# The fifth row tile of layer 2 in two column halves of 64 rows, with the next 64 rows behind a branch

## The chip, the cores and the metric

The kernel runs on one core of one Trainium2 chip. The metric is the device time of that core in microseconds; before the change it is 227.52 us, the median of three runs (227.28 to 228.74). The profile is of one further execution, whose span is 224.6 us; positions in time are counted from the start of that span.

## The reference

Two stages follow each other. The first is a linear attention over q, k and v of shape 8 x 8 x 576 x 64 (batch, heads, positions, width): q is softmaxed over its width, k over its positions, and the result is q (k^T v) for each head. The second takes the 4608 rows of 512 numbers that come out and sends each through one of eight experts, picked by a hash of its token:

```
q_s = exp(q - max(q, -1)) ; q_s /= sum(q_s, -1)
k_s = exp(k - max(k, 2))  ; k_s /= sum(k_s, 2)
kv  = einsum('bhsd,bhse->bhde', k_s, v)
x   = einsum('bhsd,bhde->bhse', q_s, kv)      -> 4608 rows of 512
expert_idx = token_ids * 2654435761 % 8
out[rows of e] = max(x[rows of e] @ w1[e], 0) @ w2[e]      (512 -> 1024 -> 512)
```

The rows of an expert are known only from the data. The inputs are one seeded draw, in which the eight experts get 631, 561, 550, 592, 536, 584, 564 and 590 rows.

## The kernel before, in words

**Attention and sorting.** For each of the eight batches the kernel loads q, k and v, exponentiates on ScalarE, forms k^T v and the attention rows on TensorE, scales them on VectorE into xn, and then sorts the rows by expert: one-hot matrices built on VectorE (line 609) multiply the rows on TensorE (619), and GpSimd copies the segments into xT (653). Each expert has room for 640 rows in xT (CAP), in two halves of 320 (H2). Which output row belongs to which slot is worked out on VectorE (lines 430 to 477; selA and selB are the operands), and a chain of 40 matmuls at line 834 sums it into an index table idx. Should an expert have more rows than fit, a flag sends all engines into a second copy of the computation, the fallback, which stands behind one branch per engine at line 154; with this draw it isn't run.

**The experts.** `layer1` (695) computes hT = relu(xT^T w1) for two of eight 128-row chunks of the hidden width at a time, for one half of the rows: 8 matmuls, into two PSUM banks out of banks 0 to 5 (`lslot`). The first half is always 320 columns wide; in the second the width of the matmul is a shape register that holds the expert's count less 320, cut to between 32 and 320 (`widths`, `load_widths`). The relu out of PSUM is on ScalarE (702) or VectorE (704). `layer2` (721) takes 128 rows of hT as the stationary operand and all 512 columns of w2 as the moving one, and sums eight chunks of the hidden width into one bank, 6 or 7 in turn: 8 matmuls of 128x512. Five such row tiles, t = 0 to 4, make an expert. The first four cover rows 0 to 511; the fifth covers rows 512 to 639, of which only the first (count - 512) hold data. `rows_out` copies a tile from PSUM to yo, on ScalarE for even t (731) and on VectorE for odd t (733), for expert 0 always on ScalarE. `store` (739) sends the 128 rows to their places in the output with one indirect DMA from GpSimd; slots without a row have an index beyond the output and are dropped.

**What sets the order.** The program is written out by hand as one list of operations per engine; each engine works its list in order. `Emit.op` collects what an operation reads (R), writes (W) and writes in part (P), works out which other engines' semaphores it must wait for, places these waits ahead of the operation's first instruction, and lets its last instruction count up its engine's semaphore. W waits for all earlier writers and readers, P for readers only. TensorE doesn't wait for itself. For each expert ee, TensorE's list reads: layer 1 of expert ee+1, two units of its first half; layer 2 of ee, five tiles; then the six other units of layer 1 of ee+1. Expert 1's layer 2 has the index table's matmuls ahead of it. The stores of the last expert come after GpSimd's branch at line 154.

So layer 2 of tile t waits for the copy of tile t - 2 out of the same bank: `layer2` writes one bank alone.

Of the kernel before, what the change touches and what calls it, by code (L numbers as in the profile page):

```python
# [9 lines left out]
ACTF = mybir.ActivationFunctionType  # L10
# [154 lines left out]
def fused_kernel(nc, q, k, v, moe_token_ids, moe_w1, moe_w2, out):  # L165
    B, H, S, DH = q.shape
    NTOK = moe_token_ids.shape[0]
    E, D, F = moe_w1.shape
    assert (B, H, S, DH, E, D, F) == (8, 8, 576, 64, 8, 512, 1024) and NTOK == B * S
    NC = 9  # L170
    T = 5
# [6 lines left out]
    H2 = CAP // 2  # L178
    CAPS = CAP + SEG[0]
    FC = F // 128  # L180
    NYO = 13

    em = Emit(nc)
# [4 lines left out]
    def at(name, shape, dt, off=None):  # L188
        size = {F32: 4, BF16: 2, F16: 2, I32: 4, I64: 8}[dt]
        for n in shape[1:]:  # L190
            size *= n
        size = (size + 31) // 32 * 32
        if off is None:
            off = cur[0]
            cur[0] += size
        return nc.alloc_sbuf_tensor_at(name, shape, dt, offset=off)
# [21 lines left out]
    hT = [at("hT%d" % i, [128, FC, CAP], BF16) for i in range(2)]  # L218
# [3 lines left out]
    w1b, w2b, wreg = [], [], [qkv0, qkv0 + 18432, qkv0 + 36864, exp0]  # L222
# [3 lines left out]
    NW = len(wreg)  # L226
    yo = [at("yo%d" % i, [128, D], F32, xn0 + 2048 * ((i - 1) % NYO)) for i in range(NYO)]
# [43 lines left out]
    PB = nc.alloc_psum_tensor("ps", [128, 8, 512], F32)  # L271
    PBH = PB[:].rearrange("p b x -> p (b x)").bitcast(BF16)
    bk = [Buf() for _ in range(8)]
# [4 lines left out]
    def dv(fn, R=(), W=(), P=()):  # L278
        em.op("dve", fn, R, W, P)

    def ac(fn, R=(), W=(), P=()):
        em.op("act", fn, R, W, P)
# [31 lines left out]
    for h in range(2):  # L314
        for a in range(2):
# [8 lines left out]
       R=[b_tok], P=[b_ei])  # L324
# [7 lines left out]
        out=flg[:], in0=e_f[:].rearrange("p b (g t) -> p (b g) t", t=TG).unsqueeze(2).to_broadcast(gs4),  # L332
        in1=iota8[:].unsqueeze(1).unsqueeze(3).to_broadcast(gs4), op=ALU.is_equal),
       R=[b_ef2, bc["iota8"]], W=[b_flg])
# [5 lines left out]
          R=[b_flg, bc["upper"], bc["ones"]], W=[bk[6], bk[7]])  # L340
# [13 lines left out]
       R=[b_pr], W=[b_pos])  # L354
# [55 lines left out]
           W=[b_wd])  # L410
        gp(lambda e: e.tensor_copy(out=widei[:], in_=wide[:]), R=[b_wd], W=[b_wi])

    shp = []

    def load_widths():
        def ld(e):
            rs = [e.alloc_register("wd%d" % i) for i in range(E)]
            e.load(rs, widei[0:1, :])
            shp.extend(e.shape_register(i) for i in range(E))
            for h in range(2):  # L420
                e.move_shape(shp[4 * h:4 * h + 4],
                             [[(1, e.snap(r, min_val=32, max_val=H2))] for r in rs[4 * h:4 * h + 4]])
        em.raw("pe", ld, R=[b_wi])
# [235 lines left out]
    b_w2 = [Buf() for _ in range(NW)]  # L659
    b_hT = [[[Buf() for _ in range(FC // 2)] for _ in range(2)] for _ in range(2)]  # L660
    b_yo = [Buf() for _ in range(NYO)]
# [3 lines left out]
    def weights1(ee, s, R=()):  # L665
        for a in range(2):
            em.dma("pool", "d_w1_%d" % s, lambda e, a=a: e.dma_start(
                w1b[s][64 * a:64 * a + 64, :, :],
                moe_w1[ee].rearrange("(a g p) f -> a p g f", a=2, g=4)[a]), R=R,
                W=([b_w1[s]] if a == 0 else ()), P=(() if a == 0 else [b_w1[s]]))  # L670
# [13 lines left out]
    def weights2(ee, s):  # L684
        for a in range(2):
            em.dma("pool", "d_w2_%d" % s, lambda e, a=a: e.dma_start(  # L686
                w2b[s][:, 4 * a:4 * a + 4, :],
                moe_w2[ee].rearrange("(c p) d -> p c d", p=128)[:, 4 * a:4 * a + 4, :]),
                W=([b_w2[s]] if a == 0 else ()), P=(() if a == 0 else [b_w2[s]]))
# [17 lines left out]
    lsl, ysl, yev = [0], [0], [0]  # L707

    def lslot():
        lsl[0] += 1  # L710
        return 2 * ((lsl[0] - 1) % 3)

    def l1(ee, f, hf, u, onact):
        layer1(ee % NW, f, hf, lambda d: xT[:, d, CAPS * ee + H2 * hf:CAPS * ee + H2 * hf + H2],
               [b_xT] if hf == 0 else [b_xT, b_x6, b_x7], ee % 2, u, onact, ee if hf else None,
               b_wf[f // (FC // 2)] if ee == 0 else None)

    def layer2(s, t, hp):
        u = 6 + ysl[0] % 2
        ysl[0] += 1  # L720
        em.op("pe", [lambda e, fc=fc: e.matmul(  # L721
            PB[:, u, :], hT[hp][:, fc, 128 * t:128 * t + 128], w2b[s][:, fc, :],
            start=(fc == 0), stop=(fc == FC - 1)) for fc in range(FC)],
            R=[b_w2[s]] + (b_hT[hp][0] if t < 3 else []) + (b_hT[hp][1] if t > 1 else []), W=[bk[u]])
        return u

    def rows_out(u, onact):
        y = yev[0] % NYO
        yev[0] += 1
        if onact:  # L730
            ac(lambda e: e.activation(yo[y][:], PB[:, u, :], ACTF.Copy), R=[bk[u]], W=[b_yo[y]])  # L731
        else:
            dv(lambda e: e.tensor_copy(out=yo[y][:], in_=PB[:, u, :]), R=[bk[u]], W=[b_yo[y]])  # L733
        return y
# [3 lines left out]
    def store(ee, t, y, after=()):  # L738
        em.dma("pool", "d_o%d" % y, lambda e: e.indirect_dma_start(  # L739
            out=out[:, :], out_offset=IndirectOffsetOnAxis(ap=idx[:, 5 * ee + t:5 * ee + t + 1], axis=0),  # L740
            in_=yo[y][:], in_offset=None, bounds_check=NTOK - 1, oob_is_err=False),
            R=[b_yo[y], b_idx, *after], P=[b_out])
# [88 lines left out]
    def index_table():  # L831
        u = lslot()
        P2 = PB[:, u, 0:2 * B * T]
        em.op("pe", [lambda e, i=i: e.matmul(P2, selA[:, i, :], selB[:, valid[i], :, :].rearrange("p k n -> p (k n)"),
                                             start=(i == 0), stop=(i == B * T - 1)) for i in range(B * T)],
              R=[b_A, b_B], W=[bk[u]])
        dv(lambda e: e.tensor_copy(out=idxf[:], in_=P2[:, B * T:2 * B * T]), R=[bk[u]], W=[b_idf])
        dv(lambda e: e.scalar_tensor_tensor(out=idxf[:], in0=P2[:, 0:B * T], scalar=64.0, in1=idxf[:], op0=ALU.mult,
                                            op1=ALU.add), R=[bk[u]], W=[b_idf])
        dv(lambda e: e.tensor_scalar(out=idxf[:], in0=idxf[:], scalar1=-1.0, scalar2=8192.0, op0=ALU.mult,  # L840
                                     op1=ALU.add), W=[b_idf])

        dv(lambda e: e.tensor_scalar(out=idx[:], in0=idxf[:], scalar1=ov8k[:, 0:1], scalar2=None, op0=ALU.max),
           R=[b_idf, b_ov8], W=[b_idx])
# [6 lines left out]
    for ee in range(E):  # L851
        units = [(f, hf) for hf in range(2) for f in range(0, FC, 2)] if ee > 0 else [(f, 1) for f in range(0, FC, 2)]
        for i, (f, hf) in enumerate(units):
            if i == 2:
                if ee == 1:
                    for key in ("pe", "pool"):
                        em.load_flag(key, ovfi[0:1, 0:1], [b_ovi])
                    index_table()
                for t in range(T):
                    y = rows_out(layer2(ee % NW, t, ee % 2), ee == 0 or t % 2 == 0)  # L860
                    if ee == E - 1:
                        em.after_tail(lambda: store(ee, t, y))
                    elif ee == 1:
                        store(0, t, t, [b_yo[y]])
                        held.append((t, y))
                    elif ee > 1:
                        if held:
                            store(1, *held.pop(0), [b_yo[y]])
                        store(ee, t, y)
                if ee == 0:  # L870
                    weights2(3, 3)
                if ee == E - 2:
                    before_last = dict(em.cnt)
                if 0 < ee < E - 3:
                    weights1(ee + 3, (ee + 3) % NW)
                    weights2(ee + 3, (ee + 3) % NW)
            if ee + 1 < E:
                l1(ee + 1, f, hf, lslot(), ee == 0 or ee == 1 and i < 2 or (f // 2) % 2)
            if ee == 1 and i in (2, 4, 6):
                store(1, *held.pop(0), [b_hT[0][hf][f // 2]])  # L880
# [40 lines left out]
    for t in range(T):  # L921
        dv(lambda e, t=t: e.tensor_copy(out=idt[:, t, 128 * t:128 * t + 128], in_=ident[:]), R=[bc["ident"]],
           W=[b_id])
    for b in range(B):
# [12 lines left out]
        for ch in range(4):  # L937
            u = 2 * (ch % 2)
            em.op("pe", [lambda e, t=t, hf=hf, ch=ch, u=u: e.matmul(
                PB[:, u + hf, 0:H2], xn[0][:, t, 128 * ch:128 * ch + 128], idt[:, t, H2 * hf:H2 * hf + H2],  # L940
                start=(t == 0), stop=(t == T - 1)) for t in range(T) for hf in range(2)],
                R=b_xn[0] + [b_id], W=bk[u:u + 2])
            ac(lambda e, ch=ch, u=u: e.activation(xg[:, ch, :].rearrange("p (h x) -> p h x", h=2),
                                                  PB[:, u:u + 2, 0:H2], ACTF.Copy), R=bk[u:u + 2], W=[b_xg[ch]])
        for ee in range(E):
# [5 lines left out]
            for t in range(T):  # L951
                u = layer2(NW, t, 2)
                m = flg[:, 2 * b + t // TG, ee, t % TG:t % TG + 1]
                if ee == 0:
                    dv(lambda e, t=t, u=u, m=m: e.tensor_scalar(out=yg[:, t, :], in0=PB[:, u, :], scalar1=m,
                                                                scalar2=None, op0=ALU.mult),
                       R=[bk[u], b_flg], W=[b_yg[t]])
                else:
                    dv(lambda e, t=t, u=u, m=m: e.scalar_tensor_tensor(
                        out=yg[:, t, :], in0=PB[:, u, :], scalar=m, in1=yg[:, t, :], op0=ALU.mult, op1=ALU.add),  # L960
                       R=[bk[u], b_flg], W=[b_yg[t]])
# [9 lines left out]
def bass_efficient_attn_shen__then__hash_routing_kernel(nc, q, k, v, moe_token_ids, moe_w1, moe_w2, out):  # L971
    fused_kernel(nc, q, k, v, moe_token_ids, moe_w1, moe_w2, out)
# [28 lines left out]
```

## Time and profile before

| | |
|---|---|
| time | 227.52 us |
| span of the profile | 224.6 us, TensorE at full clock |
| TensorE matmul busy | 193.6 us (86%), 1786 matmuls |
| VectorE / ScalarE / GpSimd busy | 126.0 / 106.4 / 120.4 us |
| layer 2 matmuls (721), 128x512 | 320, in stretches of 40 |
| layer 1 matmuls (695), second half up to 320 wide | 512 |
| a yo copy of 128x512, ScalarE / VectorE | 597 ns / 692 ns, 26 and 14 of them |
| a relu of 128x640, ScalarE / VectorE | 703 ns / 824 ns |

Busy time of the matmuls includes their pipeline: one of 512 columns is shown as 379 ns but the next starts 216 ns after it, and this start-to-start time (the slot) is what a row of them costs. In a line of the timeline the columns are start, length, engine, line, operation, output and inputs; in brackets is how long the engine had stood idle, and what released it. A line of the chain of work has start, length, and engine, tile and line. "PE" is TensorE, "DVE" VectorE, "ACT" ScalarE, "POOL" GpSimd, and "ps" is PSUM.

### The profile page before, as it was taken

Reading aid. Unit: us, or ns where it says so; the run is one execution under the profiler, and the core shown is the slowest. Engines: PE = TensorE matmul, PEld = TensorE weight load, DVE = VectorE, ACT = ScalarE, POOL = GpSimd, SP = SyncE. Lnnn points to the kernel's source line nnn. Section 1 sums busy time; section 2 is a strip of 40 time slices with the busy share of each in tenths; the row PEclk is TensorE's granted clock in tenths of the full one; section 3 lists DMA queues with packets and bytes.
Section 4 is the critical chain, followed back from the end, with each engine's and each line's share of the span. In section 5 each row is a group of like instructions: output and inputs, shape, how many; then the busy total and the mean of one; then the engine's idle time right before and its main releaser. Section 6 shows DMA issues by size and latency. Waiting matters only on the chain.

```text
span 224.6 us, 4635 instructions
## 1 busy us (share of the span) xinstructions
PE 193.6 (86%) x1786; PEld 130.8 (58%) x1788; DVE 126.0 (56%) x276; ACT 106.4 (47%) x133; POOL 120.4 (54%) x226
## 2 busy tenths in 40 slices
PE   0529976967777799999989999999999999999991
PEld 0328665856565667774654854854855845845640
DVE  5777999988898975899932412412421422412220
ACT  3447887888878837673521331331322322322411
POOL 6600658887996999910005857806715615126053
PEclk9999999999999999999999999999999999999999
DMA  5999999999999999999995599999799799113023
GB/s 144 400 392 393 388 390 390 391 391 395 387 390 392 281 176 186 204 210 206 210 208 157 146 191 228 357 192 237 200 207 258 143 206 228 73 40 147 26 93 134
DMA packets 29791, 54.96 MB, mean 245 GB/s; under 512 B 2367, under 2 KB 11583, under 8 KB 29760
## 3 DMA queue, kind: packets, MB, share of 16 engines
q0 software_dynamic: 16544, 26.22, 56.2%
q1 hardware_dynamic: 13216, 28.35, 34.3%
q8 instruction: 16, 0.26, 0.5%
q14 instruction: 15, 0.12, 0.2%
HBM read 61.90 MB, written 10.49 MB: 322 GB/s over the span
## 4 chain that ended last, share of the span: by engine, by line
PE 49%; DVE 21%; DMA 15%; SPq 9%; issue 3%; ACT 1%; POOL 1%; DVEq 0%; POOLq 0%
PE ps L721 26%; PE ps L695 20%; SPq L495 8%; DMA kf<-in_k_dram 7%; DMA vf<-in_v_dram 7%; DVE selA L477 3%; DVE xn L596 3%; DVE vx L514 1%; DMA tok<-in_moe_token_ids_dram 1%; DVE xT L653 1%; DVE oneh L609 1%; DVE selB L465 1%; DVE zz L433 1%; DVE selB L468 1%; ACT ek L509 1%
## 5 line engine op out<-in xcount | busy, mean ns | idle before, releaser
L739 POOL DMA_INDIRECT out_dram<-yo,idx x40 | 39.5, 988 | 75.5 <-ACT yo L731 55.4
L721 PE MATMUL ps<-w2b,hT 128*128 128x512 bf16 x320 | 70.4, 379 | 0.0
L695 PE MATMUL ps<-xT,w1b 128*128 128x320 bf16 (+1 forms) x512 | 64.4, 286 | 0.3 <-DVE xn L596 0.3
L695 PEld LDWEIGHTS ps<-xT,w1b 128*128 128x128 bf16 x512 | 49.8, 98 | 14.5 <-DVE xn L596 0.7
L721 PEld LDWEIGHTS ps<-w2b,hT 128*128 128x128 bf16 x320 | 31.3, 98 | 36.2
L653 POOL COPY xT<-xs x112 | 45.0, 455 | 9.3 <-issue 2.3
L702 ACT ACTIVATE hT<-ps 128x640 bf16<-128x640 f32 x41 | 28.8, 703 | 36.2 <-PE ps L695 35.9
L731 ACT ACTIVATE yo<-ps 128x512 f32<-128x512 f32 x26 | 15.5, 597 | 55.2 <-PE ps L721 55.2
L704 DVE TENSOR_SCALAR hT<-ps 128x640 bf16<-128x640 f32 x23 | 19.0, 824 | 30.2 <-PE ps L695 30.2
L733 DVE COPY yo<-ps 128x512 f32<-128x512 f32 x14 | 9.7, 692 | 44.0 <-PE ps L721 44.0
L619 PE MATMUL ps<-oneh,xn 128*128 128x384 bf16 (+1 forms) x160 | 22.8, 297 | 3.9 <-DVE xn L596 3.9
L596 DVE TENSOR_TENSOR xn<-ps,rq 128x1024 bf16<-128x1024 f32 (+2 forms) x23 | 23.6, 1079 | 3.3 <-PE ps L591 3.3
L505 ACT ACTIVATE eq<-qf 128x1152 bf16<-128x1152 f32 x16 | 17.7, 1156 | 11.3 <-DMA qf<-in_q_dram 11.3
L619 PEld LDWEIGHTS ps<-oneh,xn 128*128 128x128 bf16 x160 | 14.6, 99 | 11.3 <-DVE xn L596 4.7
L626 ACT ACTIVATE xs<-ps 128x768 bf16<-128x768 f32 (+1 forms) x32 | 18.7, 651 | 3.3 <-PE ps L619 2.7
L509 ACT ACTIVATE ek<-kf 128x2304 bf16<-128x2304 f32 x8 | 17.0, 2123 | 6.4 <-DMA kf<-in_k_dram 6.4
L591 PE MATMUL ps<-kvn,qT 128*128 128x128 bf16 x160 | 11.3, 231 | 5.2 <-DVE kvn L555 5.1
L546 PE MATMUL ps<-vx,ek 64*128 64x130 bf16 x252 | 9.4, 229 | 6.5 <-DVE vx L514 6.5
L523 PE MATMUL ps<-ident,eq 128*128 128x128 bf16 x144 | 11.4, 242 | 3.2 <-ACT eq L505 2.3
L591 PEld LDWEIGHTS ps<-kvn,qT 128*128 128x128 bf16 x160 | 9.9, 104 | 6.0 <-DVE kvn L555 5.7
L546 PEld LDWEIGHTS ps<-vx,ek 64*128 64x128 bf16 x252 | 8.3, 100 | 7.9 <-issue 5.2
L686 POOL DMA_DIRECT2D w2b<-in_moe_w_dram x16 | 12.3, 793 | 0.0
(105 smaller groups left out, 139.1 us busy)
## 6 DMA issues: line engine op xcount, KB each, us to landing
qf<-in_q_dram SPq DMA_DIRECT2D x8, 1152.0 KB, 15.5
kf<-in_k_dram SPq DMA_DIRECT2D x8, 1152.0 KB, 15.7
w2b<-in_moe_w_dram POOLq DMA_DIRECT2D x16, 512.0 KB, 11.7
vf<-in_v_dram SPq DMA_DIRECT2D x7, 1152.0 KB, 15.4
w1b<-in_moe_w_dram POOLq DMA_DIRECT2D x14, 512.0 KB, 8.4
vf<-in_v_dram SPq DMA_DIRECT2D x2, 576.0 KB, 14.7
w1b<-in_moe_w_dram POOLq DMA_DIRECT2D x4, 256.0 KB, 6.0
out_dram<-yo,idx POOLq DMA_INDIRECT x40, 3.8
```

The costliest lines, as they stand in the source:

```text
L495: em.dma("sync", nm % p, lambda e, dst=dst, src=src: e.dma_start(dst[p][:].rearrange("p h c d -> p h (c d)"), src[b].rearrange("(a h) (p c ...
L509: ac(lambda e: e.activation(ek[p][:].rearrange("p j c a d -> p a (j c) d"), kf[p][:].rearrange("p (a j) c d -> p a (j c) d", a=2), ACTF.Ex ...
L591: em.op("pe", [lambda e, i=i, j=j, h2=h2: e.matmul(PB[:, bank + i, 256 * j + 128 * h2:256 * j + 128 * h2 + 128], qt(p, t0 + i, j, h2), kvn ...
L596: dv(lambda e: e.tensor_tensor(out=xn[p][:, t0:t0 + n, :].rearrange("p t (g x) -> p (t g) x", x=DH), in0=PB[:, bank:bank + n, :].rearrange ...
L619: em.op("pe", [lambda e, g=g, i=i, k=k, n=n: e.matmul(PB[:, bank + k, 0:GW[0]] if g == 0 else PB[:, one, GW[1] * k:GW[1] * (k + 1)], xn[p] ...
L626: ac(lambda e, g=g, src=src: e.activation(xs[p][:, c0:c0 + 2, XO[g]:XO[g] + GW[g]], src, ACTF.Copy), R=bs, P=b_xs[p][c0:c0 + 2])
L653: return e.tensor_copy(out=xT[:, :, bass.ds(do, SEG[g])], in_=xs[p][:, :, XO[g]:XO[g] + GW[g] + SEG[g]][:, :, bass.ds(so, SEG[g])])
L695: em.op("pe", [lambda e, d=d, k=k: e.matmul(cut(PB[:, u + k, 0:H2]), w1b[s][:, d, 128 * (f + k):128 * (f + k) + 128], cut(rhs(d)), start=( ...
L702: ac(lambda e: e.activation(o, i, ACTF.Relu), R=bk[u:u + 2], W=[b_hT[hp][hf][f // 2]])
L704: dv(lambda e: e.tensor_scalar(out=o, in0=i, scalar1=0.0, scalar2=None, op0=ALU.max), R=bk[u:u + 2], W=[b_hT[hp][hf][f // 2]])
L721: em.op("pe", [lambda e, fc=fc: e.matmul(PB[:, u, :], hT[hp][:, fc, 128 * t:128 * t + 128], w2b[s][:, fc, :], start=(fc == 0), stop=(fc == ...
L739: em.dma("pool", "d_o%d" % y, lambda e: e.indirect_dma_start(out=out[:, :], out_offset=IndirectOffsetOnAxis(ap=idx[:, 5 * ee + t:5 * ee + ...
```

## The change

The fifth tile is no longer computed as 128 rows by 512 columns. It is split in two groups of 64 rows. A group is computed in two column halves that lie in different column groups of the TensorE array: columns 0 to 255 of the 64 rows come out on PSUM partitions 0 to 63, columns 256 to 511 on partitions 64 to 127, of one bank. Each half needs 8 matmuls of 256 columns, issued in turn with the other half's. The first group (rows 512 to 575) is always computed, into bank `ua`; the second (rows 576 to 639), into bank `ub`, only if the expert's second half is wider than 256, which is tested on TensorE with a register loaded with the widths. In the program the branch stands first and the always-computed group after it. Four copies instead of one take the result to yo: two on ScalarE for rows 0 to 63 and two on VectorE for rows 64 to 127. The purpose is that halves in different column groups can run side by side, so that 64 rows take half of the time of a full tile, and that the second 64 rows needn't be computed where an expert has none.

The operation declares both banks as written, `W=[bk[6], bk[7]]`. The first four tiles, layer 1 and the stores stay as they are.

```diff
+            wreg_pe.extend(rs)
...
+    def layer2_rest(ee):
+        s, hp, c0, y = ee % NW, ee % 2, 512, yev[0] % NYO
+        yev[0] += 1
+        ua, ub = 6 + ysl[0] % 2, 6 + (ysl[0] + 1) % 2
+        DHF = D // 2
+
+        def part(e, u, r, fc, j):
+            return e.matmul(PB[64 * j:64 * j + 64, u, DHF * j:DHF * j + DHF], hT[hp][:, fc, r:r + 64],
+                            w2b[s][:, fc, DHF * j:DHF * j + DHF], start=(fc == 0), stop=(fc == FC - 1))
+
+        def more(e):
+            with e.If(e.snap(wreg_pe[ee], min_val=32, max_val=H2) > c0 + 64 - H2):
+                for fc in range(FC):
+                    for j in range(2):
+                        part(e, ub, c0 + 64, fc, j)
+        em.op("pe", [more] + [lambda e, fc=fc, j=j: part(e, ua, c0, fc, j) for fc in range(FC) for j in range(2)],
+              R=[b_w2[s]] + b_hT[hp][1], W=[bk[6], bk[7]])
+        for j in range(2):
+            o, r = slice(DHF * j, DHF * j + DHF), slice(64 * j, 64 * j + 64)
+            ac(lambda e, o=o, r=r: e.activation(yo[y][0:64, o], PB[r, ua, o], ACTF.Copy), R=[bk[ua]], P=[b_yo[y]])
+            dv(lambda e, o=o, r=r: e.tensor_copy(out=yo[y][64:128, o], in_=PB[r, ub, o]), R=[bk[ub]], P=[b_yo[y]])
+        return y
...
-                    y = rows_out(layer2(ee % NW, t, ee % 2), ee == 0 or t % 2 == 0)
+                    y = layer2_rest(ee) if t == T - 1 else \
+                        rows_out(layer2(ee % NW, t, ee % 2), ee == 0 or t % 2 == 0)
```

More of the change, by code (lines that the diff above doesn't have):

```diff
@@ L411, in widths @@
         gp(lambda e: e.tensor_copy(out=widei[:], in_=wide[:]), R=[b_wd], W=[b_wi])
-    shp = []
+    shp, wreg_pe = [], []
     def load_widths():
```

## The prediction

> **What bounds the kernel now.** I read the busy slices first, then the chain of work that ended last, TensorE's waits, and the timeline around one fourth row tile and around the end.
>
> ```profile
> PE   0529976967777799999989999999999999999991
> DVE  5777999988898975899932412412421422412220
> PEclk9999999999999999999999999999999999999999
> ```
>
> Counted from 0, a slice being 5.6 us, TensorE is at 9 tenths or more from slice 21 (118 us) to the last but one, at full clock, and VectorE at 1 to 4 tenths. The chain, cut to the stretch around and after that, in columns start, length, what:
>
> ```profile
> 107.05 6.52 DVE selA L477 x40
> 113.57 0.05 issue
> 113.62 1.61 PE ps L834 x40
> 115.22 8.63 PE ps L721 x40
> 123.86 7.49 PE ps L695 x64
> 131.35 8.63 PE ps L721 x40
> 139.99 8.05 PE ps L695 x64
> ...
> 205.50 5.85 PE ps L695 x48
> 211.36 6.92 PE ps L721 x32
> ...
> 218.30 0.70 DVE yo L733
> ```
>
> Up to 113.57 VectorE sets the end, with the rows of the index table; from 113.62 it is TensorE alone, alternating layer 2 (L721: 40 matmuls, five tiles) and layer 1 (L695). A tile is 8.63 / 5 = 1.73 us, a matmul 216 ns. TensorE's only wait from 85 us on is
>
> ```profile
> PE ps L834 <- DVE selA L477: 0.9, 1, 0.9
> ```
>
> So a time added to or taken from layer 2 of experts 1 to 7 goes straight into the total; for expert 0, whose layer 2 runs at 100 to 108.7 us, the first 1.07 us vanish in that wait (0.91 as the view shows, plus 0.16 by which the modelled end of the last layer 1 matmul, 299 ns, exceeds its slot, 136).
>
> Two evictions, the fourth tile of expert 1 and, further down, of expert 7 with what follows:
>
> ```profile
> 122.17 0.69 DVE L733 COPY yo<-ps 128x512 f32<-128x512 f32 x1 [2.76 <-PE ps L721]
> ...
> 218.30 0.69 DVE L733 COPY yo<-ps 128x512 f32<-128x512 f32 x1 [2.76 <-PE ps L721]
> 219.79 0.97 POOL L739 DMA_INDIRECT out_dram<-yo,idx  x1 [0.85 <-DVE yo L733]
> 220.03 0.60 ACT L731 ACTIVATE yo<-ps 128x512 f32<-128x512 f32 x1 [2.86 <-PE ps L721]
> 221.42 0.97 POOL L739 DMA_INDIRECT out_dram<-yo,idx  x1 [0.66 <-issue]
> ```
>
> The fourth tile's last matmul starts at 121.75, so its slot ends at 121.97; VectorE copies from 122.17 to 122.86. Today the fifth tile's matmuls run through this, because they go to the other bank.
>
> [...] The trace has no column tiles; it has row tiles (L546, 64 of 128 rows), where a pair of 130-column matmuls takes 58 ns, hardly more than one would, so independence holds there. [...] the branch at L154 (over the fallback code) took 45 ns on SyncE with the next instruction 0.50 us after its start, but 2.8 us to the next on ScalarE, 2.9 on VectorE, and 4.01 us by itself on TensorE, whose fallback is long.
>
> **The change part by part.**
>
> *Which experts take the branch.* It is taken when the second-half width exceeds 256. Widths follow from layer 1's time: expert 2's 7.49 us less 32 matmuls of 320 columns (32 x 0.136) leaves 98 ns for each of 32, and (98 - 2.5) x 2.4 columns/ns is 230 (2.4 and 2.5 from 512 columns in 216 ns and 80 in 36). Expert 3's 8.05 gives 272. Counting the seeded draw of the reference gives 311, 241, 230, 272, 216, 264, 244 and 270 for experts 0 to 7. So 0, 3, 5 and 7 take it and 1, 2, 4 and 6 skip it.
>
> *Removed per expert:* the fifth tile's 8 matmuls, 1.73 us.
>
> *The new wait.* The new operation declares that it writes both banks, 6 and 7. Bank 7 holds the fourth tile, so TensorE's queue stands until VectorE's copy is done: slot end 121.97 to copy end 122.86, plus 0.05 from a released semaphore to the weight load (as at 113.57), 0.95 us. Behind it in TensorE's queue stand the fifth tile and all of the next layer 1, which nothing else can start; ScalarE's and VectorE's next relus wait for those. Expert 0's fourth tile is copied by ScalarE in 0.60, so 0.85 there.
>
> *The branch*, exposed because it comes after that wait with an empty array. Register move to branch is 0.10 us in L154's records[...]. When it falls through (taken body) I take 0.2. A skip jumps some 32 instructions: at least 0.15, and by SyncE's jump 0.10 + 0.50 = 0.6; I take 0.4.
>
> *The matmuls.* A group of 64 rows is 16 matmuls of 256 columns in eight pairs. One is 256 / 2.4 + 2.5 = 109 ns. Perfect pairs: 8 x 0.109 = 0.88; nothing shared: 1.75. [...] I take 0.95. A skipping expert runs one group, a taking one two (1.90), which is no less than the old tile.
>
> *Going back to full width* for layer 1: from L546 to L581 the trace shows 143 ns from start to start where a slot is 56, so 0.1 (0 to 0.15).
>
> *Evictions.* One ScalarE copy of 0.60 becomes two there and two on VectorE, 64x256 each. ScalarE's rows (492 ns at 384 columns, 597 at 512) give 0.385 each; VectorE's nearest row (64x256, L555) is 0.42. About 0.9 us on each engine, in parallel. In experts 0 to 6 they lie beside the next layer 1 unit (8 x 0.136 = 1.09 us), whose relus come after it and whose banks rotate over three slots: nothing. In expert 0 VectorE's two stand behind selA, and bank 7 isn't needed until 1.7 us into expert 1's layer 2: nothing. In expert 7 the last store waits for them: two copies plus the 0.12 by which two relus in a row (1.53 us) exceed 2 x 0.70 is 0.89, so +0.29. The looser order on yo and the registers kept for the widths cost nothing: they add no instruction.
>
> Sum, in us:
> - skipping, 1, 2, 4, 6: 0.95 + 0.40 + 0.95 + 0.10 - 1.73 = +0.67, four times 2.68
> - taking, 3 and 5: 0.95 + 0.20 + 1.90 + 0.10 - 1.73 = +1.42, twice 2.84
> - expert 7: 0.95 + 0.20 + 1.90 - 1.73 + 0.29 = +1.61
> - expert 0: 0.85 + 0.20 + 1.90 + 0.10 - 1.73 = 1.32, less the 1.07 of slack, +0.25
>
> Together +7.4: 227.5 + 7.4 = 234.9. With every unknown at its cheap end (skip and fall-through 0.15, group 0.88, mode 0) it is 4 x 0.25 + 2 x 1.13 + 1.42 + 0 = 4.7, 232.2.
>
> **The rivals.**
> 1. *Halves don't overlap* (a group 1.75). Each of the 4 + 8 groups costs 0.80 more, +9.6: 244.5. For it: [...] both halves need all 128 rows of the array. Against: the row pairs of L546 overlap almost wholly. Half an overlap would be about 239.
> 2. *The wait costs nothing*, the change pays where the branch is skipped. Without the 0.95s the central sum is 7.4 - 7 x 0.95 - 0.25 = +0.5 (228.0); with the cheap ends 4 x (-0.70) + 2 x 0.18 + 0.47 = -2.0 (225.5). Its middle, 226.8, is not slower than before. For it: VectorE is idle 2.76 us before the copy, so it starts at once. Against: copy and semaphore are a chain with no work of TensorE's own in front.
> 3. [...] 2.9 us as on VectorE instead of 0.4, four times: +10, 244.9; with TensorE's 4.0 up to 249. One miss alone gives about 238. For it: the far jumps at the end. Against: the target is 32 instructions on, and SyncE's short jump took 0.5.
>
> **How the numbers follow.** Forecast 0.72; half an overlap or a single miss 0.09; rival 1 0.10; rival 2 0.04; rival 3 0.05. The range runs from the cheap end, 232.2 less 0.6 for scatter (the three times before spread over 1.5), to 241, which takes in half an overlap and one miss and leaves out the three rivals, 0.19. Slower by over 1% means above 229.8: 0.94. Rival 2 is split: same 0.04 with the fringe of the forecast, faster 0.02.
>
> **What would show it.** TensorE should show a wait of its matmuls for VectorE's yo copy of about 0.9 us in experts 1 to 7; groups of 16 matmuls spaced 109 ns a pair; layer 2 stretches of 9.3 us for experts 1, 2, 4, 6 and 10.0 for 3 and 5 against 8.63; the wait at L834 all but gone; and the last store some 7 us later. A TensorE gap well over 1.3 us before a fifth tile would be the branch; a group of 1.7 us would be rival 1; no gap would be rival 2. I am wrong most likely in the price of the skip and in the pairs' overlap, neither of which this trace shows.

## The result, and the profile after

The changed kernel takes 234.66 us, the median of four runs (234.31 to 236.10), beside 228.13 us for the kernel before on the same chip. The ratio is 1.0291, with an interval of 1.0231 to 1.0351: 6.6 us slower, between 5.3 and 8.0. The forecast was 234.9. A ratio, here and below, is taken over the runs within 1.5% of their kernel's fastest; that leaves runs out in two of the experiments, and these have the median of all runs beside it.

The profile is of the longest of the four, 236.10 us, with a span of 234.3 us. First the busy slices of TensorE; a slice is now 5.9 us:

```profile
PE   0539797887777898998997997998998989989970
```

Where there was a row of nines there is now an 8 or a 7 in about every third slice, once for each expert. TensorE's waits from 85 us on (tile and line, what released it, then total us, number, longest) say what stands there:

```profile
PE ps L737 <- DVE yo L759: 7.6, 7, 1.3
PE ps L696 <- DMA w1b<-in_moe_w_dram: 0.9, 1, 0.9
PE ps L737 <- ACT yo L757: 0.9, 1, 0.9
PE ps L696 <- DVE hT L705: 0.4, 1, 0.4
```

The first and third rows are the fifth tile, eight times out of eight, waiting for the copy of the fourth: VectorE's in experts 1 to 7, ScalarE's in expert 0. These times run to the group's first matmul, so the branch behind the copy is in them. The old wait for selA is gone: TensorE now reaches the index table at 114.97, after VectorE has finished (113.67). The chain of work shows what an expert looks like, first one that skips the branch (expert 2), then one that takes it (expert 3):

```profile
133.45 6.87 PE ps L722 x31
140.32 0.02 issue
140.34 0.70 DVE yo L759
141.04 0.39 issue
141.43 1.06 PE ps L737 x16
...
151.27 6.87 PE ps L722 x31
158.14 0.02 issue
158.16 0.70 DVE yo L759
158.87 0.25 issue
159.12 1.94 PE ps L737 x32
161.05 7.41 PE ps L696 x64
```

Before, TensorE was the only engine in this part of the chain. Now VectorE's copy of 0.70 us sits in it, and behind the copy 0.39 us (0.25 when the body runs) in which the register is moved and the branch decided. In TensorE's records the branch itself takes 70 ns when it falls through into the body (96 in expert 0) and 202 to 222 ns when it jumps over it. The 16 matmuls of a group then take 1.06 us by their modelled ends; in the records, start to start, the eight pairs are 109.3 ns apart after a first step of 125 to 134, so a group takes 0.875 us. The group itself is as cheap as the purpose of the change wanted.

These two rows of costliest groups show that the weight loads are no hindrance either (busy time, mean ns of one, idle time before):

```profile
L737 PE MATMUL ps<-w2b,hT 128*64 128x256 bf16 x192 | 12.0, 274 | 8.5 <-DVE yo L759 7.6
L737 PEld LDWEIGHTS ps<-w2b,hT 128*64 128x64 bf16 x192 | 9.9, 110 | 12.4 <-issue 12.4
```

A load of 64 columns is recorded with 110 ns, which is a whole pair's time, with two of them to a pair; the pairs keep to 109.3 ns all the same. At the end, the timeline of the copies and of the last store:

```profile
228.15 0.78 ACT L749 ACTIVATE yo<-ps 64x256 f32<-64x256 f32 x2 [4.05 <-PE ps L737]
228.16 0.87 DVE L750 COPY yo<-ps 64x256 f32<-64x256 f32 x2 [2.24 <-PE ps L737]
229.82 0.97 POOL L765 DMA_INDIRECT out_dram<-yo,idx  x1 [2.13 <-DVE yo L750]
```

The last store is issued 1.71 us after the last matmul's modelled end (228.12 to 229.82), where it was 1.43 before (219.99 to 221.42): +0.28.

### The profile page after: what moved, and what is told of

Read it like the earlier page. It is cut to its first block, busy times and chain, and to the rows that moved or that the text cites. A ratio compares the mean times of both kernels' runs of the same rounds, so it can differ in the third digit from the quotient of the medians.

```text
span 234.3 us, 4944 instructions
## 1 busy us (share of the span) xinstructions
PE 192.8 (82%) x1906; PEld 134.4 (57%) x1916; DVE 132.8 (57%) x292; ACT 108.1 (46%) x141; POOL 120.8 (52%) x226
## 4 chain that ended last, share of the span: by engine, by line
PE 56%; POOL 14%; DVE 9%; issue 8%; DMA 5%; POOLq 3%; ACT 2%; DVEq 0%; ACTq 0%
PE ps L696 25%; PE ps L722 23%; POOL xT L654 11%; PE ps L737 5%; DMA w1b<-in_moe_w_dram 4%; DVE yo L759 2%; POOLq L652 2%; POOLq L646 2%; DVE xn L597 1%; DMA tok<-in_moe_token_ids_dram 1%; DVE oneh L610 1%; ACT xs L627 1%; PE ps L547 1%; POOL gx L369 1%; PE ps L860 1%
## 5 line engine op out<-in xcount | busy, mean ns | idle before, releaser
L696 PEld LDWEIGHTS ps<-xT,w1b 128*128 128x128 bf16 x512 | 49.0, 98 | 16.1 <-issue 1.4
L722 PE MATMUL ps<-w2b,hT 128*128 128x512 bf16 x248 | 54.8, 379 | 0.4
L722 PEld LDWEIGHTS ps<-w2b,hT 128*128 128x128 bf16 x256 | 24.9, 98 | 28.8
L757 ACT ACTIVATE yo<-ps 128x512 f32<-128x512 f32 x18 | 10.8, 598 | 33.0 <-PE ps L722 33.0
L749 ACT ACTIVATE yo<-ps 64x256 f32<-64x256 f32 x16 | 6.1, 379 | 29.7 <-PE ps L737 21.6
L737 PE MATMUL ps<-w2b,hT 128*64 128x256 bf16 x192 | 12.0, 274 | 8.5 <-DVE yo L759 7.6
L737 PEld LDWEIGHTS ps<-w2b,hT 128*64 128x64 bf16 x192 | 9.9, 110 | 12.4 <-issue 12.4
L592 PE MATMUL ps<-kvn,qT 128*128 128x128 bf16 x160 | 12.4, 243 | 4.8 <-DVE kvn L556 4.7
L750 DVE COPY yo<-ps 64x256 f32<-64x256 f32 x16 | 6.8, 423 | 14.8 <-PE ps L737 10.2
```

The source lines that it names most:

```text
L696: em.op("pe", [lambda e, d=d, k=k: e.matmul(cut(PB[:, u + k, 0:H2]), w1b[s][:, d, 128 * (f + k):128 * (f + k) + 128], cut(rhs(d)), start=( ...
L722: em.op("pe", [lambda e, fc=fc: e.matmul(PB[:, u, :], hT[hp][:, fc, 128 * t:128 * t + 128], w2b[s][:, fc, :], start=(fc == 0), stop=(fc == ...
L737: return e.matmul(PB[64 * j:64 * j + 64, u, DHF * j:DHF * j + DHF], hT[hp][:, fc, r:r + 64], w2b[s][:, fc, DHF * j:DHF * j + DHF], start=( ...
```

## The experiments

**Theory.** The loss is the wait that the declaration of both banks brings, seven times 0.95 us, with the branch exposed behind it; the 64-row groups are not at fault. **Rivals.** The branch or the jump is what costs; or the column halves, the way into them and back, or their copies are. In all runs below the ratio is to the kernel before on the same chip, and "us" from a ratio is (ratio - 1) x 228.

**wait_alone**: the kernel before, with one bank more declared for its fifth tile and nothing else.

```diff
-            ..., W=[bk[u]])
+            ..., W=bk[6:8] if hp < 2 and t == T - 1 else [bk[u]])
```

> The kernel before, with the fifth tile declaring both banks as written and nothing else. If the new wait carries the loss, TensorE stands 0.95 us before the fifth tile of experts 1 to 7 and expert 0's 0.85 vanishes in the slack at the index table: +6.6 us, ratio about 1.029. If the wait is hidden and the branch, the column halves or the four copies cost the time, no more than 1 us, ratio within 1.005.

Measured: 1.0308 [1.0277, 1.0339], +7.0 us. Its waits on TensorE:

```profile
PE ps L721 <- DVE yo L734: 5.6, 7, 0.9
```

One stretch of layer 2 went from 8.63 to 9.59 us, so a wait is 0.96: the 0.80 of the view and the 0.16 by which the modelled end of a 512-column matmul (379 ns) exceeds its slot (216). The full old tile, no branch, no column halves, and the whole loss is there. The wait is enough to make it; what the rest of the change pays and gains must then nearly cancel.

**both_no_branch**: the changed kernel without the condition; both groups are always computed.

```diff
-            with e.If(e.snap(wreg_pe[ee], min_val=32, max_val=H2) > c0 + 64 - H2):
-                for fc in range(FC): ...
+            for fc in range(FC): ...
```

> The changed kernel with both groups of 64 rows always computed and no branch. Against the changed kernel the four skipping experts gain a group of 0.875 us each (+2.6 for the three that count besides expert 1, +3.5 in all) and lose the skip's 0.35; the taking ones lose the branch's 0.2: +3.5 - 1.4 - 0.6 = +1.5 us against the changed kernel, ratio to before about 1.035. If the branch were the main cost, [...] it would be faster than the changed kernel: ratio below 1.02.

Measured: 1.0389 [1.0356, 1.0423], +8.9 us. Slower than the change by some 2 us, so the branch saves more than it costs, and the first rival falls. A layer 2 stretch is 9.63 us here (133.63 to 143.26).

**slot_banks**: the fifth tile's groups go to a pair of layer 1's banks, so no wait for banks 6 and 7 is left.

```diff
-        ua, ub = 6 + ysl[0] % 2, 6 + (ysl[0] + 1) % 2
+        ua = lslot()
+        ub = ua + 1
...
-              R=[b_w2[s]] + b_hT[hp][1], W=[bk[6], bk[7]])
+              R=[b_w2[s]] + b_hT[hp][1], W=[bk[ua], bk[ub]])
```

> The changed kernel with the two groups in a pair of layer 1's banks instead of 6 and 7, so that nothing has to be copied out before the fifth tile starts. If wait and branch are what costs, both vanish from TensorE's path (the queue runs ahead of the array): skipping experts 0.875 + 0.1 - 1.73 = -0.75 four times, taking ones +0.12 twice, the last +0.4: -2.3 us, ratio about 0.990. If the branch costs its 0.2 to 0.35 even without the wait, ratio about 0.998. If the column halves or the copies were the cost, about the changed kernel's 1.029.

Measured: 1.0281 [1.0228, 1.0334], +6.4 us: a miss. The waits at L738 are gone, but two others have come, first in the list of waits, then in the chain:

```profile
PE ps L696 <- DVE yo L751: 3.7, 1, 3.7
PE ps L696 <- DVE hT L705: 2.9, 1, 2.9
```

```profile
107.17 6.51 DVE selA L478 x40
113.70 0.42 DVE yo L751
114.12 0.03 issue
114.16 0.44 DVE yo L751
114.59 0.14 issue
114.73 3.77 PE ps L696 x16
```

Expert 0's copies on VectorE are queued behind the rows of selA, until 113.70. In bank 6 or 7 that hurt nobody; in a bank of layer 1 they hold up layer 1 of expert 1, and through it the index table. Expert 1's layer 2 starts at 119.99 instead of 115.22. The second wait, in expert 2, is another matter and comes back below under the name of **late start**: ScalarE and VectorE begin an operation up to 4.1 us after the matmuls that they wait for are over by the record (144.53 and 148.59 here). Not all of the 3.77 us of the chain is due to the wait: TensorE's granted clock was 0.50 from 114.30 to 117.70.

**first_group_ahead**: 14 of the always-computed group's 16 matmuls are put ahead of the wait, as an operation that writes only its own bank; branch and the last pair follow.

```diff
+        em.op("pe", [lambda e, fc=fc, j=j: part(e, ua, c0, fc, j) for fc in range(FC - 1) for j in range(2)],
+              R=..., W=[bk[ua]])
+        em.op("pe", [more] + [lambda e, j=j: part(e, ua, c0, FC - 1, j) for j in range(2)],
+              R=..., W=[bk[ua], bk[ub]])
```

> The changed kernel with 14 of the 16 matmuls of the first group issued ahead of the wait for bank 7, and the branch and the last two behind it. They take 0.77 us of the 0.95 that TensorE stands: -0.77 seven times against the changed kernel, -5.4 us, ratio to before about 1.006. If the stall isn't the wait for bank 7, no change against the changed kernel, 1.029.

Measured: 1.0205 [1.0167, 1.0244], +4.7 us: better than the change, but less than expected. Expert 3 in the chain:

```profile
159.46 0.89 PE ps L737 x14
160.34 0.11 issue
160.46 1.17 PE ps L737 x18
```

The stall has shrunk from 0.70 + 0.25 to 0.11 us (0.25 where the branch is skipped), as meant. The rest went to a late start in expert 2: from the end of its layer 2 (140.05 in TensorE's records) to the next layer 2 (152.55) are 12.50 us, where 8.16 are due (the 8.05 of before and 0.11 for the return to full width).

**before_again**: the kernel before, unchanged, to see how much two runs of the same program differ.

> The kernel before, unchanged, as the control for the traces. In the changed kernel, and in all four kernels run so far, ScalarE and VectorE start some operations of expert 2 (140 to 149 us) 0.5 to 3.4 us after what they wait for. If that belongs to the kernel's own transfers at that point, it shows here too; if the longer fifth tile brings it on, no operation of the control is late there. Time: no difference.

Measured: 1.0008 [0.9990, 1.0026]. Its profile has a late start too: layer 1 in expert 2 took 8.63 us (140.68 to 149.31) instead of 8.05. So the late start isn't made by the change; it is there before, at 0 in one profile and 0.6 us in the other.

**slot_banks_e1**: slot_banks, with expert 0's fifth tile left as before.

```diff
-                    y = layer2_rest(ee) if t == T - 1 else \
+                    y = layer2_rest(ee) if t == T - 1 and ee > 0 else \
```

> As the version with the groups in layer 1's banks, but expert 0's fifth tile as in the kernel before, so that no copy of a bank that layer 1 needs next stands on VectorE behind the rows of the index table. If that was the 3.7 us that TensorE waited there, they are gone: ratio from 1.028 to about 1.012. If the late start in expert 2 goes as well, about 0.990.

Measured: 1.0038 [1.0016, 1.0061], +0.9 us; its runs spread from 227.08 to 232.07 us, and the median of all 20 is 228.96, +1.1 us. The wait of 3.7 us is gone, and with it 5.5 us; no wait stands ahead of a fifth tile. In the chain, experts 1 and 3:

```profile
115.47 6.91 PE ps L722 x32
122.37 0.99 PE ps L738 x16
123.37 7.60 PE ps L696 x64
...
149.03 6.91 PE ps L722 x32
155.93 1.87 PE ps L738 x32
```

Layer 2 is 7.90 us where the branch is skipped and 8.77 where it is taken, against 8.63: the branch costs nothing any more, since TensorE's queue is ahead of its array there and decides it while earlier tiles' matmuls are still running (119.82 to 120.08 in expert 1, during the third tile).

**slot_both_e1**: the same without the branch (both groups always), banks as in slot_banks_e1.

> As the last, but both groups always computed and no branch: the column halves alone, in a place without a new wait. 1.75 + 0.1 - 1.73 = +0.12 us for experts 1 to 6, +0.4 for the last: +1.1 us, ratio about 1.005, plus up to 3 us (1.018) if the late start in expert 2 stays. Against the version with the branch +0.875 for each of the four that skip, +3.5 us in all, if the branch is hidden behind the queue.

Measured: 1.0152 [1.0111, 1.0193], +3.5 us, 2.6 us more than with the branch. The four groups left out are worth 4 x 0.875 = 3.5 us; the two intervals, 0.5 and 0.9 us either way, are wide enough for the rest.

**copies_alone**: the kernel before, with the fifth tile copied in four pieces of 64x256, two on each engine, and nothing else changed.

> The kernel before, with the fifth tile copied out by four copies of 64x256, two on ScalarE and two on VectorE, and nothing else. If they lie beside layer 1 as worked out, only the last store is later, +0.3 us, ratio within 1.005. If the copies were part of the loss, up to 0.9 us for each of seven experts, 1.02 or more.

Measured: 1.0063 [1.0045, 1.0082], +1.4 us, over the 0.3 that was expected. 0.17 of it is the later last store (1.60 us after the last matmul, 1.43 before); the profile's only new wait is a late start in expert 2 (9.37 us, 140.30 to 149.67, instead of 8.05). So the copies don't make the loss.

**one_bank**: both groups in one bank of the two that layer 2 had, 6 and 7 in turn. A group's halves take partitions 0 to 63 and 64 to 127, so the other group's halves fit on the opposite partitions; the four copies follow them there.

```diff
-        ua = lslot()
-        ub = ua + 1
+        u = 6 + ysl[0] % 2
+        ysl[0] += 1
...
-                        part(e, ub, c0 + 64, fc, j)
+                        part(e, 1 - j, c0 + 64, fc, j)
-        em.op("pe", [more] + [... part(e, ua, c0, fc, j) ...], R=..., W=[bk[ua], bk[ub]])
+        em.op("pe", [more] + [... part(e, j, c0, fc, j) ...], R=..., W=[bk[u]])
```

> The changed kernel with both groups in one bank: the second group's halves lie on the other halves of the partitions, where the first leaves its bank free, and the copies are shared out so that ScalarE reads partitions 0 to 63 and VectorE 64 to 127. The bank turns as in the kernel before, so nothing new is waited for and layer 1 keeps its slots. From the traces: skipping experts 7.90 + 0.11 against 8.63, -0.62 four times; taking ones 8.78 + 0.11, +0.26 twice; the last +0.15 and its copies +0.3: -1.5 us, ratio about 0.993. If the copies on both engines or the late start in expert 2 cost about 1 us, ratio 0.998; if the wait was not the cause at all, 1.029.

Measured: 1.0032 [1.0003, 1.0060], a miss. Its runs spread from 226.90 to 232.08 us; the median of all 22 is 230.07, +2.0 us. The profiled run took 230.55. No wait is left ahead of L738, but the late start is there (12.91 us from 139.05 to 151.96, where 8.16 are due), and TensorE's granted clock was halved after it (0.50 from 146.00 to 149.40). "Another core or an unknown queue" is the profile's name for a releaser that it can't place. Columns of the second fence: stretch, length, busy us of PE, PEld, DVE, ACT and POOL each with their instructions, granted clock, DMA share, GB/s.

```profile
140.88 3.38 another core or an unknown queue
145.17 6.80 PE ps L696 x40
```

```profile
146.00:149.40 3.40, 3.40 (x18) 2.28 (x16) 0.82 (x1) 0.70 (x1) 0.00 (x0) 0.50 1.05 195
```

The same 40 matmuls take 5.13 us in the changed kernel at full clock.

**one_bank_inner**: one_bank for experts 1 to 6 alone; 0 and 7 as before.

> As the last, but experts 0 and 7 keep the fifth tile of the kernel before: neither can gain, the first because its time is absorbed at the index table, the last because it takes the branch and its copies stand before the last store. Against the last version -0.45 us and the later last store (about -0.5): ratio about 0.990. No difference to the last version if the end isn't set by the copies.

Measured: 1.0053 [1.0030, 1.0076], +1.2 us: a miss again, and again by the late start:

```profile
131.05 6.85 PE ps L722 x31
137.91 2.00 PE ps L738 x16
139.90 0.02 issue
139.93 0.43 DVE yo L751
140.35 0.03 issue
140.38 0.42 DVE yo L751
140.81 3.41 another core or an unknown queue
```

The group of 16 really takes 0.99 us and was over at 138.90; the copies that it releases started 1.03 us later, and the relu after them at 144.24. It is TensorE's signal that is late, not the two engines. The trace records each count of TensorE's semaphore: four here stand at 139.90, 144.22, 144.31 and 144.41, for matmuls that were over at 138.90, 140.09, 141.18 and 142.11, while in the trace of before no such count from 90 us to the last matmul comes over 0.06 us after its matmul's end. VectorE started 0.02 us after the second of them.

**no_weights_4**: the kernel before without expert 4's weight loads, which are in flight at that time. Expert 4's rows are computed with expert 0's weights. There is one run.

> The kernel before without the loads of expert 4's weights, which run from 126 to 142 us (expert 4's rows are then computed with the weights that lie in the slot, those of expert 0). The time is read for the late start of ScalarE and VectorE in expert 2 alone. If the transfers of that stretch bring it on, no operation there starts over 0.25 us late and the wait of 0.4 us of the control is gone; if it stays, the cause lies elsewhere.

Measured: 229.18 us. The late starts are still there (2.31 us after the matmuls on ScalarE, 1.47 on VectorE). These loads don't make them.

**inner_no_store_1**: one_bank_inner without the five stores of expert 1; the output rows of expert 1 are not written.

```diff
                     elif ee == 1:
                         store(0, t, t, [b_yo[y]])
-                        held.append((t, y))
```

> The one-bank version with experts 0 and 7 as before, with the five stores of expert 1 left out (its rows of the output aren't written). Those stores run from 129 to 137 us, ahead of expert 2's, in front of the late start of ScalarE and VectorE at 140 to 144. If the scattered stores bring the late start on, it goes, and TensorE's wait of 3.0 us for a relu with it: ratio to before about 0.988. If it stays, the ratio stays at 1.005 and the cause stays open.

Measured: 225.05 us, 0.9910 [0.9891, 0.9928], -2.1 us. No late start in the profile; TensorE has no wait left but the one for selA:

```profile
138.08 0.99 PE ps L738 x16
139.07 8.16 PE ps L696 x64
```

In one_bank_inner the scattered stores leave GpSimd every 1.28 us without a pause from 134.2 to 142.8 us; here there are five in that time. So without this burst, the late start isn't there. But the burst alone doesn't make it: the first trace of before has the same seven stores, one each 1.28 us from 134.50 to 143.14, and no count of TensorE's is late in it. Since this kernel stores less, it isn't a version of the same computation, and no kernel run here that computes everything beats the one before.

**The runs, added up.** Per expert, on the start-to-start times above, and with column halves plus 0.11 us for the return to full width (an expert that skips the branch 7.90 against 8.63, so -0.73 + 0.11 = -0.62; one that takes it 0.14 + 0.11 = 0.25):

| kernel | sum from its own profile, us | from the ratio, us |
|---|---|---|
| wait_alone | 7 x 0.96 + late start 0.46 = 7.2 | 7.0 [6.3, 7.7] |
| both_no_branch | 6 x (1.00 + 0.11) + expert 7 (1.00 + 0.28) + late start 0.96 = 8.9 | 8.9 [8.1, 9.6] |
| slot_banks_e1 | 4 x (-0.73 + 0.11) + 2 x (0.14 + 0.11) + expert 7 (0.16 + 0.28) + late start 2.0 = 0.5 | 0.9 [0.4, 1.4] |
| slot_both_e1 | 6 x (0.14 + 0.11) + expert 7 (0.16 + 0.28) + late start 1.7 = 3.6 | 3.5 [2.5, 4.4] |
| copies_alone | last store 0.17 + late start 1.32 = 1.5 | 1.4 [1.0, 1.9] |
| one_bank_inner | 4 x (-0.62) + 2 x 0.25 + late start 3.2 = 1.2 | 1.2 [0.7, 1.7] |
| inner_no_store_1 | 4 x (-0.62) + 2 x 0.25 = -2.0 | -2.1 [-2.5, -1.6] |

The late start is the lengthening of expert 2's stretch of layer 1 over its 8.05 us, or over 8.16 with column halves. It is read from one profile of each kernel, and it differs from run to run (0 and 0.6 us for the kernel before), so sums and ratios agree more closely than this can promise. Expert 0's longer layer 2 is left out: the slack of 1.07 us ahead of the index table takes it. The stretches of experts 1 and 2 stand for the others of their kind. The last row leaves nothing for the missing stores as such: they matter by the late start alone. What holds TensorE's signal back during a burst of stores in one execution and not in another stays open. Spreading these stores, with none left out, wasn't tried.

## Why the prediction was right, by its steps

- **The new wait, 0.95 us.** Right: 140.32 to 141.04 in the chain plus the 0.16 by which a modelled end exceeds its slot is 0.88, or 0.93 with the 0.05 of the release; it is 0.96 in wait_alone. There, alone, it makes a loss as large as the whole change's, and slot_banks_e1, without it, is about 1 us from before. TensorE's queue held nothing ahead of it that could have run, as the prediction said; only a rewrite could put work there, as first_group_ahead did with 14 of the tile's own matmuls.
- **The branch, 0.20 or 0.40.** 0.25 and 0.39 us between copy and first matmul, of which 0.05 is the release that is counted with the wait: 0.20, and 0.34 (0.46 once, in expert 1). No skip was a miss in the forecast's sense, 2.9 us instead of 0.4: the longest jump took 0.22 us, so rival 3 is out. The branch by itself is 70 to 96 ns into the body and 202 to 222 past it; in the trace of before the one at L154 took 45 to 72 ns on the four engines other than TensorE.
- **The group, 0.95.** 0.875: mis-sized by 0.08. The 0.95 was an estimate, with an allowance above the 0.88 of perfect pairs; the pairs, 109.3 ns apart, needed next to none. Rival 1 is out.
- **Return to full width ("mode" in the forecast), 0.10.** 0.11: the layer 1 stretch of 7.49 us became 7.60. The trace shows the time, not what it is spent on. (From L546 to L581 the records of before have 147 or 148 ns, once 243, not 143.) Going in costs as much (0.99 for a group in slot_banks_e1 against 0.875), but the wait hid it in the changed kernel.
- **The last copies, +0.29.** 0.28.
- **The experts.** Layer 2 of a skipping expert took 9.09 (2, 4, 6) and 9.23 us (1), so with the 0.11 it lost 0.57 and 0.71, where 0.67 was forecast. A taking one took 9.83: 1.31 lost, 1.42 forecast. Expert 7: 1.5 against 1.61. Expert 0's layer 2 took 9.76; 1.13 and 0.11, less the slack of 1.07, make 0.17 against 0.25. Together 3 x 0.57 + 0.71 + 2 x 1.31 + 1.5 + 0.2 = 6.7 us; forecast 7.4, measured 6.6. The term that was too dear is the group: 12 of them, 0.075 each, are 0.9. With the late start of 0.6, below, the parts make 7.3. That 234.9 lies only 0.2 from 234.66 is in part luck: the forecast of the loss was 0.8 too high, and the kernel before took 0.6 us more beside the change than the 227.52 it started from.
- **The spans differ by more**, 9.7 us. The profiled execution was the longest of the changed kernel's (236.10 us), and that of before, at 226.3, was shorter than any of its timed ones here. Besides the 6.7, its layer 2 of expert 0 began 1.2 us later (a wait for w1b, 0.9, is part of it), expert 2 had 0.6 of late start, and from the last store's issue to the end of the span it was 1.3 us longer. So the last store came 8.4 us later, where some 7 were forecast.
- **What the forecast didn't see.** It spoke of rival 2, the wait hidden, at 226.8 us. one_bank_inner is close to that case and gave 229.15: the late start took the gain and 1.2 us more. The trace of before had none to show. In the changed kernel it cost 0.6 us, since the new waits spread the stores out too; that reason is argued, not shown.

## What to carry to other kernels

Before you split a tile, ask which buffer its new pieces declare: a second bank that was written a moment ago puts the eviction of the tile ahead of it on the path, and this cost more here (0.96 us an expert) than the split gained where it gained (0.62 us in four experts). Here a branch behind such a wait was paid in full (0.25 us into the body, 0.38 to 0.51 past it), and one behind running matmuls was free (in slot_banks_e1 the group follows the fourth tile without a gap, at 122.37 in the chain). After removing a wait, look in the new profile for the next one, and set its size against the gain before you judge the idea.

## What the runs showed of the hardware that was not expected

- Two matmuls of 256 columns in different column halves of the array overlap entirely: 109.3 ns a pair, the second 3 to 12 ns after the first, though each one's 64-column weight load is recorded with 110 ns.
- Both groups of 64 rows fit into one bank, on opposite partition halves, with no price in time (0.99 and 1.87 us, as in two banks).
- In 12 of the 14 profiles, in expert 2, TensorE's semaphore counts came late behind a burst of scattered stores, one each 1.28 us: up to 4.1 us after the matmul's end, then two or three of them 0.09 us apart. With five of the stores left out none was late. One trace of the kernel before has the burst and no late count, so the burst alone isn't enough.
- TensorE stood for 2.5 to 3.7 us in three profiles (first_group_ahead, one_bank, and slot_banks ahead of 114.73) and its granted clock was halved for 3.4 us (0.50 in one_bank and slot_banks, 0.52 over 3.5 us in first_group_ahead), from 0.4 us before its next matmul in slot_banks and from 0.4 and 0.8 us after it in the others: there 40 matmuls took 6.80 instead of 5.13 us. Stands of 3.0 in one_bank_inner and 2.9 in slot_banks (expert 2) left the clock alone. In one_bank the 3.4 us before the halving still held 0.8 us of matmuls (145.17 to 146.00). What decides whether a stand halves the clock isn't shown.
